# Retention and masked expert attention: the attention of each tile one step later, the projections spread over three steps, the output tiles moved

## The chip, the cores and the metric

The kernel runs on one core of one Trainium2 chip. The metric is the time of one execution on the device in microseconds (us), lower is better; the median of three runs before the change is 471.17 us (469.44 to 471.55). The engines have short names in the rows: PE is TensorE (matmuls; PEld its weight loads), DVE is VectorE, ACT is ScalarE, POOL is GpSimd, SP issues the DMAs.

## The reference

Two layers follow one another. The first is retention, causal attention without softmax, for 8 batches, 8 heads, 576 tokens and a head width of 64. The second takes its output (576 tokens, width 512) through four experts, each a causal softmax attention of width 64, and sums the two experts that a gate picks for each token.

```
scores = scale * (q @ k.T) * Dmat          # Dmat[i, j] = gamma_h ** (i - j) for j <= i, else 0
x = (scores @ v), heads side by side       # (8, 576, 512)

logits = x @ w_gate                        # 4 experts, best 2 kept, softmax over the 2
for e in range(4):
    q, k, v = x @ wq[e], x @ wk[e], x @ wv[e]
    a = softmax(causal(scale * q @ k.T))
    out += weight_of(e) * (a @ v @ wo[e])  # weight 0 where e is not picked
```

## The kernel before

The loop has 37 steps, n = 0 to 36. One step makes 128 rows of retention output for one pair of batches; nine steps (a period) make a pair, so there are four periods. Each engine runs its instructions strictly in the order in which the program emits them. There are 8 PSUM banks, handed out in turn: a new matmul result takes the bank that was handed out eight results earlier, and PE waits until that one was copied out.

A step emits, in this order. `factors` of the tiles scored one step earlier (DVE: softmax sum, reciprocal, times the gate's weight). `qk(n)` (two banks, copied out by ACT at L127, masked by POOL at L130). `result(n - 1)` and `state(n)`: PE makes `old` (two banks, copied out by ACT at L153), `own` (two banks, added by DVE at L171) and `st` (two banks, added by DVE at L113). What `own` gave goes through POOL (L176, L181) and ACT (L179), which split it into a high part `xh` and a low part `xl`, the input of the second layer. Then `scores` of this step's tiles: PE fills the banks `ss` (L352, L358), DVE takes the row maxima (L367, L371), ACT first scales the tiles of the step before (L393) and then does the exponentials (L375). Only after them does ACT come to `xh` (L179) of this step. Then `gates(0)` (first half of a gate, DVE and one ACT exponential), and at last the step's share of `work`, with the transposes (`turn`, DVE, L401 and L403) of the tiles scored one step earlier beside it.

A tile (b, t) is 128 rows of batch b in the second layer, t = 0 to 4. Tables say which step does what. `TILES` gives the tiles to score. `STEPS` gives the work, and its kinds are

- `kq` (R, p): the key and query projections of the block R of 384 rows for the expert pair p, 24 matmuls `pj` (L224). They read `xh` and `xl` of three steps; there are three blocks in a period
- `v` R: the value projection, three units of 12 matmuls `pv` (L249) that also give the gate's logits
- `back`: DMAs that bring values back in another layout
- `y` b: the attention times the values for a whole batch (`values`, `ys`, L415, four banks at a time, copied out by ACT L421 and DVE L422). In a step with a `y` the transposes are held until its end, because they write what `y` reads
- `o` c: one output tile (`outproj`, `po`, L437, one bank). ACT copies it out (L443), or DVE where c is in `FAST` (L441)

A gate has two halves: `gates(0)` after the scores of a step, `gates(1)` (L303 to L312, DVE) at the end of the step. The `factors` of the tiles need the gate's weights. After step 36 `tail` finishes the last pair by hand. I write steps by their residue: step 0 of a period is n = 9, 18, 27, 36.

Of the kernel before, what the change touches and what calls it, by code (L numbers as in the profile page):

```python
# [23 lines left out]
NP = B // 2  # L24
NC = 9 * NP
NB = 384

LAG = 6


def f(ap):
    return ap.bitcast(F32)
# [3 lines left out]
def kernel(ctx: ExitStack, tc: tile.TileContext, xf, vkf, wraw,  # L36
# [161 lines left out]
    def weights(n, parts="hl"):  # L198
        o, kc, w = WCUT[n]
        raw = RAW[n]  # L200
        wt = w if n != "v" else NWV
        if "h" in parts:
            W[n] = [const.tile([128, kc, wt], F32R, name="w" + y + n) for y in "hl"]
        hi, lo = W[n]
        for r, cs in [(raw, slice(0, w))] + ([(rg, slice(w, wt))] if n == "v" else []):
            if "h" in parts:
                act(hi[:, :, cs], r, AF.Copy)
            if "l" in parts:
                (gp if n == "q" else v).tensor_sub(lo[:, :, cs], r, f(hi[:, :, cs]))

# [235 lines left out]

    FAST = {9 * P_ + c for P_ in range(NP) for c in (1, 2, 3)}

# [3 lines left out]
    for P_ in range(NP):  # L452
        b, n = 2 * P_, 9 * P_
        for t in range(5):
            TILES.setdefault(n + 6 + t, []).append((b, t))
            TILES.setdefault(n + 10 + max(t, 1), []).append((b + 1, t))

        def add(m, *w):
            STEPS.setdefault(n + m, []).extend(w)
        R = 3 * P_  # L460
        add(4 - (P_ == 0), ("kq", R, 0))
        add(5 - (P_ == 0), ("kq", R, 1))
        add(5, ("v", R))
        add(7, ("kq", R + 1, 0))
        add(8, ("kq", R + 1, 1), ("v", R + 1))
        add(9, ("kq", R + 2, 0))
        add(10, ("kq", R + 2, 1), ("v", R + 2))
        add(8, ("back", R))
        add(10, ("back", R + 1))
        add(13, ("back", R + 2))  # L470
        add(12, ("y", b))
        add(13, ("o", n))
        add(15, *[("o", n + c) for c in (1, 2, 3)])
        add(16, ("y", b + 1))
        add(18, ("o", n + 4))
        add(20, ("o", n + 5), ("o", n + 6))
        add(21, ("o", n + 7), ("o", n + 8))
    for n in STEPS:
        first = "o" if n % 9 == 0 else "k"
        STEPS[n].sort(key=lambda x: (x[0][0] != first, "kvyob".index(x[0][0])))  # L480

    def work(n):
# [3 lines left out]
        i = 0  # L486
        for kind, *w in todo:
# [10 lines left out]
            elif kind == "v":  # L498
                for t in range(3):
                    yield from vproj(w[0], t)  # L500
            elif kind == "o":
                for y in vals:
                    next(y, None)
                yield from outproj(w[0])
# [6 lines left out]
    def run(g):  # L511
        for _ in g:
            pass
# [11 lines left out]
    def tail():  # L525
# [3 lines left out]
        def outs(*cs):  # L529
            for c in cs:  # L530
                yield from outproj(c)

        factors(b, 3)
        soft = scores((b, 4))
# [5 lines left out]
        beside(proj(R, "q", 1), turns)  # L540
        gates(0)
        gates(1)
        factors(b, 4)
        soft = scores((b + 1, 0), (b + 1, 1))
        next(soft)
        run(scale(b, 4))
        back(R - 1)
        beside(vproj(R, 0), soft)
        beside(vproj(R, 1), soft)
# [54 lines left out]
    for n in range(NC + 1):  # L604
        if n < LAG:
            load(n + 2)
        if n == 1:
            nc.sync.dma_start(rg, wraw[:, 4096:].rearrange("p (k w) -> p k w", k=4))
            nc.sync.dma_start(mask[:, 448:], con_d[:, 92:])
        if n in (1, 4):  # L610
            fetch("v" if n == 1 else "o")
        late = result(n - 1) if 1 <= n <= NC else iter(())
        now, old = TILES.get(n, []), TILES.get(n - 1, [])
        for x in old:
            factors(*x)
# [24 lines left out]
        run(late)  # L640
        for w in {2: "kq", 3: "v", 6: "o"}.get(n, ""):
            weights(w, "l" if w == "k" else "hl")
# [5 lines left out]
        run(turns)  # L648
        gates(1)
    tail()  # L650
# [52 lines left out]
```

## Time and profile before

| what | value |
|---|---|
| median of 3 runs | 471.17 us |
| profiled execution, whole | 474.0 us |
| its span, first to last instruction | 472.2 us |
| PE busy | 415.5 us, 88% |
| ACT, DVE, POOL busy | 279.8, 273.8, 170.4 us |
| granted TensorE clock, mean | 0.941 |

The profile is of one execution. "Busy" is the time in which an engine ran at least one instruction. The granted clock is the share of TensorE's full speed (2.4 GHz) that the chip gave; the two levels in the rows are 1.00 and 0.50 (1.2 GHz). In a row of the timeline the bracket behind an instruction tells how long its engine sat idle before it and what ended the idle time.

### The profile page before, as it was taken

To read this page: it belongs to the slowest core of one execution; us is meant where nothing else is said; L and a number is where in the kernel's file an instruction comes from. 1 tells how busy PE (TensorE), PEld (TensorE's weight loads), DVE (VectorE), ACT (ScalarE), POOL (GpSimd) and SP (SyncE) were. 2 spreads that over 40 slices of the span, in tenths; PEclk is the share of its full clock that TensorE was granted. 3 is DMA by queue.
4 is the path that set the end of the run, shared out by engine and by line. 5 is a ranking of instruction groups with operands and counts; after the bars stand their busy time and mean duration, and the time that the engine had idled before them with its cause. 6 is when DMAs were issued, how large, how long until landed. Compare 5 with 4: busy or idle time off the path is not lost.

```text
span 472.2 us, 20318 instructions
## 1 busy us (share of the span) xinstructions
PE 415.5 (88%) x8724; PEld 350.4 (74%) x8724; DVE 273.8 (58%) x1113; ACT 279.8 (59%) x798; POOL 170.4 (36%) x183
## 2 busy tenths in 40 slices
PE   6579796996899997997899998997999999899774
PEld 3469685995798786986698787895789678787563
DVE  2852765557775465657485564558385753673840
ACT  2545496566666366567495466568396456575651
POOL 1517673344354343344254433344264522100000
PEclk9669899898899999898999999899999999899988
DMA  8836654363444354454364444355264321313311
GB/s 285 325 92 226 214 144 138 111 148 117 121 151 147 136 144 140 136 153 150 111 207 121 162 143 134 107 145 196 91 177 134 117 64 35 89 58 110 118 68 47
DMA packets 33689, 65.10 MB, mean 138 GB/s; under 512 B 3392, under 2 KB 19264, under 8 KB 33600
## 3 DMA queue, kind: packets, MB, share of 16 engines
q1 hardware_dynamic: 33600, 63.80, 42.9%
q8 instruction: 69, 1.13, 1.0%
q14 instruction: 20, 0.16, 0.1%
HBM read 49.63 MB, written 14.16 MB: 135 GB/s over the span
## 4 chain that ended last, share of the span: by engine, by line
PE 67%; DVE 17%; ACT 9%; issue 4%; DMA 2%; POOL 0%; SPq 0%; DVEq 0%; ACTq 0%
PE pj L224 24%; PE ys L415 13%; PE pv L249 10%; PE po L437 6%; PE ss L352 4%; PE qk L124 3%; ACT p L375 3%; DVE p L367 2%; DVE x L171 2%; DVE s L113 2%; PE own L166 2%; PE st L106 2%; ACT x L153 2%; DVE ta L401 2%; DMA vk<-vkf 2%
## 5 line engine op out<-in xcount | busy, mean ns | idle before, releaser
L130 POOL TENSOR_SCALAR_AFFINE_SELECT p<-p 64x512 f32<-64x512 f32 x72 | 49.4, 687 | 120.0 <-ACT p L127 117.3
L375 ACT ACTIVATE p<-p,nm 128x64 f32<-128x64 f32 (+5 forms) x144 | 79.2, 552 | 15.6 <-DVE nm L367 9.8
L393 ACT ACTIVATE p<-p,sm 128x64 f32<-128x64 f32 (+5 forms) x144 | 69.4, 563 | 26.3 <-DVE sm L387 16.0
L171 DVE TENSOR_TENSOR x<-x,own 128x256 f32<-128x256 f32 (+1 forms) x72 | 25.5, 387 | 71.6 <-ACT x L153 70.9
L181 POOL TENSOR_TENSOR xl<-x,xh 128x512 fp32r<-128x512 f32 x33 | 42.3, 1283 | 61.0 <-ACT xh L179 61.0
L176 POOL TENSOR_TENSOR x<-x,gi 128x512 f32<-128x512 f32 x33 | 42.7, 1295 | 33.8 <-ACT p L393 18.1
L422 DVE TENSOR_TENSOR yl<-ys,yh 128x288 fp32r<-128x288 f32 (+2 forms) x36 | 12.8, 417 | 67.5 <-ACT yh L421 67.5
L367 DVE CUSTOM_DVE_ANT_0 p<-ss,mask 128x128 f32<-128x128 f32 (+7 forms) x128 | 50.6, 451 | 0.9 <-PE ss L352 0.8
L415 PE MATMUL ys<-ta,vq 32*64 32x192 f32 (+5 forms) x1152 | 43.0, 383 | 8.8 <-DVE x L171 6.3
L401 DVE STREAM_TRANSPOSE ta<-p 128x256 f32<-128x256 f32 (+2 forms) x144 | 49.0, 367 | 0.9 <-ACT p L393 0.9
L415 PEld LDWEIGHTS ys<-ta,vq 32*64 32x64 f32 x1152 | 31.8, 144 | 20.6 <-DVE x L171 8.8
L352 PE MATMUL ss<-k,q 64*64 64x512 f32 (+7 forms) x512 | 41.6, 423 | 3.4 <-ACT p L127 3.4
L224 PE MATMUL pj<-xh,whk 128*128 128x384 f32 x96 | 26.6, 405 | 14.4 <-ACT xh L179 14.4
L224 PEld LDWEIGHTS pj<-xh,whk 128*128 128x128 f32 x96 | 18.0, 214 | 27.0 <-ACT xh L179 16.8
L106 PE MATMUL st<-vk 64*64 64x64 f32 x1024 | 26.8, 228 | 7.2 <-DVE vk L95 2.7
L166 PE MATMUL own<-p,vk 64*64 64x64 f32 x1152 | 28.0, 228 | 5.6 <-issue 5.5
L253 ACT ACTIVATE vn<-pv 128x260 f32<-128x260 f32 x36 | 13.7, 386 | 30.9 <-PE pv L249 29.9
L127 ACT ACTIVATE p<-qk 128x256 f32<-128x256 f32 x72 | 23.8, 384 | 13.2 <-PE qk L124 12.5
L95 POOL TENSOR_TENSOR vk<-vk,con 128x512 f32<-128x512 f32 x30 | 31.5, 1050 | 0.0
L106 PEld LDWEIGHTS st<-vk 64*64 64x64 f32 x1024 | 22.5, 141 | 8.7 <-DVE ot L441 2.9
L166 PEld LDWEIGHTS own<-p,vk 64*64 64x64 f32 x1152 | 24.1, 140 | 6.4 <-issue 6.2
L124 PE MATMUL qk<-x 64*64 64x64 f32 x1152 | 26.3, 228 | 2.6 <-issue 2.6
(86 smaller groups left out, 906.9 us busy)
## 6 DMA issues: line engine op xcount, KB each, us to landing
x<-xf SPq DMA_DIRECT2D x36, 512.0 KB, 4.3
vk<-vkf SPq DMA_DIRECT2D x36, 512.0 KB, 5.8
vq<-hv SPq DMA_DIRECT2D x48, 192.0 KB, 6.7
out<-ot SPq DMA_DIRECT2D x36, 256.0 KB, 2.2
hv<-vn SPq DMA_DIRECT2D x24, 192.0 KB, 3.5
ta<-wraw SPq DMA_DIRECT2D x4, 512.0 KB, 8.0
gi<-gi SPq DMA_DIRECT2D x1, 256.0 KB, 7.9
con<-con SPq DMA_DIRECT2D x1, 46.0 KB, 3.0
```

Source lines behind the costliest of these rows:

```text
L106: mm(ps[r][HALF[g], s, u], vk[HALF[r], s, 1, h], vk[HALF[r], s, 0, h], start=True, stop=True)
L130: gp.affine_select(w, w, pattern=[[0, 8], [1, 64]], base=0, channel_multiplier=-1, compare_op=OP.is_ge, fill=0.0)
L166: mm(own[r][HALF[u], g, i], vk[HALF[r], s, 0, 2 * g + u], p[HALF[r], g, s, u], start=True, stop=True)
L176: e.tensor_mul(x32, x32, gi[:, :, t0:t0 + 128])
L224: mm(ps, ww[:, kc, p * 128:(p + 1) * 128], xx[:, kc], start=(i == 0), stop=(i == 11))
L249: mm(ps, xx[:, kc, l0:l0 + 128], ww[:, kc], start=(i == 0), stop=(i == 11))
L352: mm(ps[u][HALF[p]], q(p, z, i), k[p][HALF[z], :ws[u]], start=True, stop=True)
L367: v.tensor_tensor_reduce(x, ps[u], mask[:, 512 - ws[u]:], -1.0, BIG, OP.add, OP.min, nm[:, u:u + 1])
L375: act(x, x, AF.Exp, bias=bias, scale=-1.0, accum_out=sm[:, 0, u:u + 1])
L393: act(x, x, AF.Copy, scale=sm[:, 1, u:u + 1])
L401: v.transpose(TA[:, :min(nb, 8), z, k], x[:, :min(nb, 8)])
L415: mm(py[g][HALF[z], sj - s0:], vq[QUAD[g], jj, D * z:D * z + D], tt[QUAD[g]], start=(j == 0), stop=(j == 2 * s1 - 1))
```

## The change

Tiles are scored one step later (`LAG`). The three `v` units of a block, which stood behind the block's last `kq`, become single entries: block R in step 6, R+1 in step 0, R+2 in steps 1 and 2; the `kq` of R+2 move from steps 0 and 1 to steps 1 and 2. `y` moves from steps 3 and 7 to steps 4 and 8, each now beside a `kq`. Output tiles move to steps 0, 3 (four of them), 5, 6 and 7. The second half of a gate is emitted at the start of the following step ahead of its `factors`, instead of at the end of the step; nothing of DVE stands between these two places. At the start of the kernel the low part of one weight moves from POOL to DVE, and the `v` and `o` weights are loaded one step later. In the last pair ACT copies out three output tiles that DVE copied, and DVE one that ACT copied. The tail gains one step of scoring and one `kq`.

```
-LAG = 6
+LAG = 7
-                (gp if n == "q" else v).tensor_sub(lo[:, :, cs], r, f(hi[:, :, cs]))
+                v.tensor_sub(lo[:, :, cs], r, f(hi[:, :, cs]))
-    FAST = {9 * P_ + c for P_ in range(NP) for c in (1, 2, 3)}
+    FAST = {9 * P_ + c for P_ in range(NP - 1) for c in (1, 2, 3)} | {NC - 2}
-            TILES.setdefault(n + 6 + t, []).append((b, t))
-            TILES.setdefault(n + 10 + max(t, 1), []).append((b + 1, t))
+            TILES.setdefault(n + LAG + t, []).append((b, t))
+            TILES.setdefault(n + LAG + 4 + max(t, 1), []).append((b + 1, t))
-        add(5, ("v", R))
+        add(5 if P_ == 0 else 6, ("v", R, 0), ("v", R, 1))
+        add(6, ("v", R, 2))
         add(7, ("kq", R + 1, 0))
-        add(8, ("kq", R + 1, 1), ("v", R + 1))
-        add(9, ("kq", R + 2, 0))
-        add(10, ("kq", R + 2, 1), ("v", R + 2))
-        add(8, ("back", R))
-        add(10, ("back", R + 1))
-        add(13, ("back", R + 2))
-        add(12, ("y", b))
-        add(13, ("o", n))
-        add(15, *[("o", n + c) for c in (1, 2, 3)])
-        add(16, ("y", b + 1))
+        add(8, ("kq", R + 1, 1))
+        add(9, ("v", R + 1, 0), ("v", R + 1, 1), ("v", R + 1, 2), ("back", R))
+        add(10, ("kq", R + 2, 0), ("v", R + 2, 0))
+        add(11, ("kq", R + 2, 1), ("v", R + 2, 1), ("v", R + 2, 2), ("back", R + 1))
+        add(13, ("y", b))
+        add(14, ("o", n), ("back", R + 2))
+        add(15, ("o", n + 1))
+        add(16, ("o", n + 2), ("o", n + 3))
+        add(17, ("y", b + 1))
         add(18, ("o", n + 4))
-        add(20, ("o", n + 5), ("o", n + 6))
-        add(21, ("o", n + 7), ("o", n + 8))
+        add(21, *[("o", n + c) for c in (5, 6, 7, 8)])
-        first = "o" if n % 9 == 0 else "k"
-        STEPS[n].sort(key=lambda x: (x[0][0] != first, "kvyob".index(x[0][0])))
+        STEPS[n].sort(key=lambda x: "kvyob".index(x[0][0]))
...
-                for t in range(3):
-                    yield from vproj(w[0], t)
+                for _ in vproj(*w):
+                    i += 1
+                    if i == 3 and bring:
+                        back(bring.pop())
+                    yield
...
+        factors(b, 2)
+        soft = scores((b, 3))
+        next(soft)
+        run(scale(b, 2))
+        run(soft)
+        gates(0)
+        turns = turn(b, 2)
+        beside(proj(R, "k", 0), turns)
+        beside(proj(R, "q", 0), turns)
+        gates(1)
         factors(b, 3)
...
-        gates(0)
-        gates(1)
+        back(R - 1)
+        run(vproj(R, 0))
         factors(b, 4)
         soft = scores((b + 1, 0), (b + 1, 1))
         next(soft)
         run(scale(b, 4))
-        back(R - 1)
-        beside(vproj(R, 0), soft)
...
-        if n in (1, 4):
-            fetch("v" if n == 1 else "o")
+        if n in (2, 5):
+            fetch("v" if n == 2 else "o")
...
+        gates(1)
         for x in old:
             factors(*x)
...
-        for w in {2: "kq", 3: "v", 6: "o"}.get(n, ""):
+        for w in {2: "kq", 4: "v", 7: "o"}.get(n, ""):
...
-        gates(1)
```

What this does to PE in step 0 of the third period (n = 18), behind the step's `st`. Before, the output tile comes first and then the projection of block R+2:

```order
L352 MATMUL ss<-k_2242,q_2802 64x448 x2
L352 MATMUL ss<-k_2243,q_2803 64x448 x2
L352 MATMUL ss<-k_2242,q_2802 64x512 x2
L352 MATMUL ss<-k_2243,q_2803 64x512 x2
L437 MATMUL po<-who,yh 128x512 x2
L437 MATMUL po<-wlo,yh 128x512 x2
L437 MATMUL po<-who,yl 128x512 x2
L224 MATMUL pj<-xh,whk 128x384 x4
L224 MATMUL pj<-xh,wlk 128x384 x4
```

After:

```order
L352 MATMUL ss<-k_2046,q_2048 64x320 x2
L352 MATMUL ss<-k_2047,q_2049 64x320 x2
L352 MATMUL ss<-k_2046,q_2048 64x384 x2
L352 MATMUL ss<-k_2047,q_2049 64x384 x2
L249 MATMUL pv<-whv,xh 128x260 x4
L249 MATMUL pv<-wlv,xh 128x260 x4
L249 MATMUL pv<-whv,xl 128x260 x4
```

The values of block R+1, whose `xh` was made in earlier steps, stand where the projection stood that reads the `xh` of this very step; two more such units and the output tile follow.

In step 3 of the same period (n = 21) before, PE goes from the scores to `y`; one step earlier it had two output tiles:

```order
L106 MATMUL st<-vk 64x64 x16
L352 MATMUL ss<-k_2800,q_3342 64x320 x2
L352 MATMUL ss<-k_2801,q_3343 64x320 x2
L352 MATMUL ss<-k_2800,q_3342 64x384 x2
L352 MATMUL ss<-k_2801,q_3343 64x384 x2
L415 MATMUL ys<-ta,vq 64x288 x16
L415 MATMUL ys<-ta,vq 64x256 x16
```

After, the same scores stand in step 4 (n = 22), and a projection's first third stands ahead of `y`; one step earlier PE has four output tiles:

```order
L106 MATMUL st<-vk 64x64 x8
L352 MATMUL ss<-k_2739,q_3432 64x320 x2
L352 MATMUL ss<-k_2740,q_3433 64x320 x2
L352 MATMUL ss<-k_2739,q_3432 64x384 x2
L352 MATMUL ss<-k_2740,q_3433 64x384 x2
L224 MATMUL pj<-xh,whk 128x384 x4
L415 MATMUL ys<-ta,vq 64x288 x16
```

So two output tiles more and a third of a projection moved in between the scores of tiles 0 and 1 and the first matmul of `y`.

## Rows read from the trace of the kernel before

**Rows 1.** The page: the span, PE's busy time, and the granted clock in 40 slices of the span (in tenths).

```profile
span 472.2 us, 20318 instructions
PE 415.5 (88%) x8724; PEld 350.4 (74%) x8724; DVE 273.8 (58%) x1113; ACT 279.8 (59%) x798; POOL 170.4 (36%) x183
PEclk9669899898899999898999999899999999899988
```

**Rows 2.** The view of waits, PE alone: what waited for what, us in total, how often, the longest.

```profile
PE pj L224 <- ACT xh L179: 14.4, 5, 4.0
PE ys L415 <- DVE x L171: 6.3, 3, 2.7
PE own L166 <- issue: 5.5, 5, 2.5
PE ss L352 <- ACT p L127: 3.4, 2, 1.9
PE st L106 <- DVE ot L441: 2.5, 3, 0.8
```

**Rows 3.** Busy time by stretch: the steps 18, 20, 21 and 25. Columns: the stretch, its length, busy time of PE, PEld, DVE, ACT, POOL (with the count of instructions), granted clock, DMA share, GB/s.

```profile
180.78:194.34 13.56, 11.18 (x176) 9.17 (x175) 8.61 (x39) 8.01 (x21) 4.86 (x5) 0.87 0.39 129
205.85:211.99 6.14, 6.14 (x173) 4.96 (x172) 4.04 (x26) 5.31 (x20) 3.60 (x4) 1.00 0.62 178
211.99:230.12 18.13, 15.66 (x446) 12.37 (x445) 9.09 (x35) 10.32 (x32) 6.13 (x6) 0.91 0.35 125
259.31:275.53 16.22, 15.37 (x458) 12.34 (x457) 7.65 (x33) 6.30 (x23) 6.15 (x6) 1.00 0.34 122
```

**Rows 4.** The timeline at step 18, around PE's wait (start, length, engine, line, operation). The first row is the same wait in step 3, at the kernel's start.

```profile
28.26 1.65 PE L224 MATMUL pj<-xh,whk 128*128 128x384 f32 x4 [3.29 <-ACT xh L179]
...
183.73 1.28 POOL L176 TENSOR_TENSOR x<-x,gi 128x512 f32<-128x512 f32 x1
186.96 0.70 ACT L375 ACTIVATE p<-p,nm 128x512 f32<-128x512 f32 x1
187.85 0.61 ACT L179 ACTIVATE xh<-x 128x512 fp32r<-128x512 f32 x1
188.52 1.65 PE L224 MATMUL pj<-xh,whk 128*128 128x384 f32 x4 [2.38 <-ACT xh L179]
```

**Rows 5.** Busy time by stretch, columns as in rows 3: stretches right behind PE's waits in the steps 9, 18 and 21.

```profile
82.50:85.80 3.30, 3.30 (x11) 3.30 (x11) 2.80 (x15) 0.00 (x0) 1.11 (x1) 0.50 0.01 2
188.30:191.60 3.30, 3.08 (x10) 3.08 (x11) 3.05 (x16) 0.65 (x2) 1.27 (x1) 0.50 0.21 82
219.00:222.30 3.30, 3.30 (x52) 2.90 (x58) 2.44 (x12) 3.30 (x11) 2.27 (x2) 0.50 0.19 74
```

**Rows 6.** The timeline from step 20 into step 21: POOL, the gate's second half on DVE, then DVE's addition of `own`, and PE's first matmuls of `y`.

```profile
213.70 1.27 POOL L181 TENSOR_TENSOR xl<-x,xh 128x512 fp32r<-128x512 f32 x1 [2.60 <-ACT xh L179]
213.82 1.18 DVE L303 SCALAR_TENSOR_TENSOR ex<-rk,ex 128x12 f32<-128x12 f32 x1
218.12 0.75 DVE L171 TENSOR_TENSOR x<-x,own 128x256 f32<-128x256 f32 x2
218.60 5.26 PE L415 MATMUL ys<-ta,vq 32*64 32x288 f32 x96 [1.81 <-DVE x L171]
219.59 0.48 DVE L367 CUSTOM_DVE_ANT_0 p<-ss,mask 128x320 f32<-128x320 f32 x1
```

**Rows 7.** The same instruction of a gate on DVE at step 18, when POOL was idle, and the end of the factors behind it.

```profile
189.60 0.24 DVE L303 SCALAR_TENSOR_TENSOR ex<-rk,ex 128x12 f32<-128x12 f32 x1
191.61 0.16 DVE L387 TENSOR_TENSOR sm<-sm,wt 128x4 f32<-128x4 f32 x1
```

**Rows 8.** The timeline at step 16: DVE copies out an output tile, PE goes on with `st`.

```profile
153.34 0.65 DVE L441 COPY ot<-po 128x512 f32<-128x512 f32 x1
154.05 0.62 PE L106 MATMUL st<-vk 64*64 64x64 f32 x26 [0.83 <-DVE ot L441]
```

**Rows 9.** The timeline at step 7: ACT prepares a weight, then copies out `qk`, then PE gets on with the scores.

```profile
53.47 1.04 ACT L207 ACTIVATE who<-ta 128x1024 fp32r<-128x1024 f32 x1
54.83 2.04 PE L352 MATMUL ss<-k,q 64*64 64x192 f32 x16 [1.90 <-ACT p L127]
```

**Rows 10.** The chain that ended last, in order of time, around step 20: one whole `kq`, one whole `v` of three units, one output tile.

```profile
197.17 4.43 PE pj L224 x24
201.60 4.32 PE pv L249 x36
223.86 1.59 PE po L437 x6
```

**Rows 11.** Code loads: the DMA queue of instructions over the whole span (packets, MB, share of 16 engines), the same in the four us from 119, and PE's wait in that stretch.

```profile
q8 instruction: 69, 1.13, 1.0%
q8 instruction: 1, 0.02, 1.8%
122.82 0.62 PE L150 MATMUL old<-x,s 64*64 64x64 f32 x25 [1.58 <-issue]
```

**Rows 12.** The timeline at step 3: POOL makes a weight's low part, DVE beside it, and the same DVE instruction of the next step.

```profile
20.30 2.45 POOL L209 TENSOR_TENSOR wlq<-ta,whq 128x1024 fp32r<-128x1024 f32 x1 [0.29 <-POOL p L130]
20.47 2.83 DVE L95 TENSOR_TENSOR vk<-vk,con 128x512 f32<-128x512 f32 x1
...
26.27 0.67 DVE L95 TENSOR_TENSOR vk<-vk,con 128x512 f32<-128x512 f32 x1
```

## The prediction

> **What bounds the kernel now.** I read the page first. PE is busy for 415.5 of 472.2 us, the other engines for 280 us or less [rows 1]: PE is the bound, and a gain must come out of the 57 us in which it waits or out of the slices in which the clock row falls below 9. The work of PE is the same before and after; the change only puts it in another order. So the question is which waits go and which come.
>
> The view of waits says for what PE waits [rows 2]. Three kinds repeat with the period. Projections `pj` wait for `xh`, 14.4 us in five waits. `y` waits for DVE's addition L171, 6.3 us in three. `st` waits for an output tile's copy on DVE, 2.5 us in three. Beside them stands "issue", a wait for nothing that the profile shows.
>
> The stretches by step place them [rows 3]. Step 18 has 13.56 us and PE is busy for 11.18; step 21 has 18.13 and 15.66; step 20 is full, but only 6.14 us long. Step lengths are that uneven while each step brings ACT and DVE about the same scores.
>
> The timeline of step 18 shows the first kind [rows 4]. POOL has the row block ready at 185.01, but `xh` stands behind the exponentials on ACT, which run until 187.66, and PE starts its projection at 188.52 after 2.38 us of waiting. The projection reads the `xh` of this very step. In steps 9, 18, 27 and 36 it is the same; with step 3's 3.29 us taken off, the four waits are 14.4 - 3.3 = 11.1 us.
>
> Then the clock [rows 5]. Behind each of these waits, and behind the `y` waits, lies a stretch with the granted clock at 0.50, that is 1.2 GHz, with PE busy nearly throughout. 3.3 us at half speed do the work of 1.65 us, so such a wait costs 1.65 us more than its row says.
>
> **The change, part by part.**
>
> *The projection of R+2 leaves step 0.* In its place stand three `pv` units, whose input was finished two steps earlier, and they take 4.32 us [rows 10]; the projection stands one step later, when `xh` is long there. The four waits go: 11.1 us, and 4 x 1.65 = 6.6 us of half clock. Term: -17.7. If the projection found another late input there, nothing would be gained; I see none, since `xh`, `xl` and the weights are all older than a step.
>
> *`y` one step later, behind four output tiles.* What makes `y` wait is DVE: scores of two tiles, half a gate, transposes, the second half of the gate and two sets of factors stand ahead of the L171 that frees the banks. L171 starts at 218.12, 12.3 us after step 20 began at 205.85 [rows 3, 6]. Step 20 has 6.14 us, so PE gets there early. After, the step with these scores has two more output tiles, 2 x 1.5 us (1.59 for one alone in [rows 10]), and lasts 9.1 us. In step 21 PE asks for the first freed bank 4.8 us after the step's start (218.60 - 1.81 - 211.99), with about 0.5 us of an "issue" wait in it; after, a projection asks for it at 9.1 + 4.3 = 13.4 us, when DVE is 1 us ahead. The later banks, which `y` needs, are ready when DVE reaches L367, 1.5 us after L171 [rows 6], and the third of a projection ahead of `y` (4.43/6 = 0.7 us) covers more of that. So the two waits of 6.3 - 2.7 = 3.6 us in steps 21 and 30 go, with two half clocks, 3.3, and half of the 1 us over which the banks of `y` came free, twice. In the first period there are no output tiles yet to lengthen the step, so the 2.7 us of step 12 stay, in step 13. Term: -7.9; bounds -9 (step 12 helped too) and -3 (only half of it, and the clock still falls).
>
> *Output tiles.* Three copies on DVE stood at the end of step 6, and `st` of step 7 waits 0.83 us for the last [rows 8]. After, one stands in step 6 and two in step 7, behind a projection. Term: -2.5; bounds 0 and -4.
>
> *First period.* In step 7 PE waits 1.90 us because ACT makes the `o` weight (1.04 us) ahead of `qk`'s copy [rows 9], and a half clock follows. After, that weight stands in a step with a whole `kq` behind the scores, 4.43 us of cover [rows 10]. Term: -1.9 - 1.65 = -3.5; without the cover nothing.
>
> *The low part of wq on DVE.* It took POOL 2.45 us, and DVE's L95, which starts beside it, took 2.83 us [rows 12]; the same instruction alone took 0.67. The Trainium skill, page "SBUF — State Buffer", section "Who interferes with whom", says that a DVE instruction with two SBUF inputs and a GpSimd instruction that reads SBUF hold the shared port in turn and the second one blocks; the rows agree, both end within 0.6 us of each other. DVE gains 2 us and takes on a subtraction that I estimate at 1.7 us, two thirds of POOL's 2.45. Term: -0.5, between 0 and -1 in a stretch that waits for other things too.
>
> *Tail.* Three copies go from DVE to ACT; DVE's transposes come 0.7 us earlier and ACT's scales a little later. Term -0.5, between +1 and -1.5.
>
> *Costs.* The `v` weights one step later on ACT and DVE, at the edge of their use in step 5: +0.4. The gate's second half keeps its neighbours on DVE, since nothing stood between its two places; but in the shorter steps around it DVE has less room: +1, bounds 0 and the first rival. The wait on the single value buffer `vn` that v's first unit in step 1 could make is covered, because the DMAs that read it started a step earlier. "Issue" waits I leave at their size (second rival).
>
> Sum: -17.7 - 7.9 - 2.5 - 3.5 - 0.5 - 0.5 + 1.4 = -31.2 us. The profiled execution took 474.0 us, 1.8 more than its span and 2.8 more than the median of the runs. 474.0 - 31.2 = 442.8; against the median, 471.2 - 31.2 = **440 us**.
>
> **Rivals.**
>
> *DVE takes over* (chance 0.15). At step 20 the first instruction of a gate's second half took 1.18 us while POOL ran L181 beside it [rows 6]; at step 18 with POOL idle it took 0.24, and from there to the end of the factors it is 2.2 us [rows 7] against 4.3 us from 213.82 to L171 at 218.12. So 2.1 us can come on top wherever POOL runs beside it. After, that piece stands at the start of steps 2, 4 and 8, always near POOL's instructions. I gave step 4 its long form already. If steps 2 and 8 get it too, and 1 us of it is covered, PE waits 1.1 us and may lose 1.65 to the clock, six times: +16, 456 us. The page's rule, by which the blocked one waits for the whole instruction, is what makes this rival; by it this is the likely form wherever the two meet. For it speaks the row, against it that DVE is less busy in step 25 (7.65 of 16.22 us) than in step 21 [rows 3].
>
> *ACT takes over* (0.08). In step 3 ACT has eight exponentials and four copies, some 10 us in a step of 9.1. If it is late, PE waits for `qk`'s copy as in step 7 and step 12 (3.4 us in two waits [rows 2]): 1.5 + 1.65 in three periods, +9.5, 449 us.
>
> *Code loads set the end, slower than before* (0.04). PE's code comes in 69 packets [rows 11]. One falls into the stretch from 119 to 123, and there PE waits 1.58 us for nothing visible. If the denser order exposed every packet, each at 0.5 us more, that would be +34.5: 474.5 us, slower by 0.7%. It decides from 0.5 us a packet. For it speaks that "issue" makes PE's third longest group [rows 2]; against it that the steps with projections run full (step 20 too), and that `y` after the change alternates with long matmuls. The Trainium skill, page "Runtime: NRT & Kernel Launch", section "Instruction fetch mechanics", says that crossing a block of code is mostly hidden; by it this rival would be nothing, but this trace shows the 1.58.
>
> *More is gained* (0.05): the "issue" waits behind `y` shrink as well and step 12's wait goes: below 431.
>
> *Nothing changes* (0.02): the removed waits were only one of two late inputs, and PE meets the second at the same time.
>
> **How the numbers follow.** The forecast has 0.66, its own range 431 to 448. With both rivals of a slow engine the range reaches to 457 and leaves out 0.05 below and some 0.08 above. A measurement of this kernel can tell 0.5% (2.4 us) from no change. Faster: 0.66 + 0.15 + 0.08 + 0.05, less 0.01 for mixtures of the rivals, is 0.93; same 0.03; slower 0.04.
>
> **What would show it.** In the profile of the changed kernel, `pj` waiting for `xh` falls from 14.4 us to about 3.3, that of step 3. The clock row has some six slices fewer below 9 after the first quarter. Steps 18, 27 and 36 are full. `y` in steps 22 and 31 starts without a wait over 1 us, and step 13 still has one near 2.7 us. `st` behind DVE's output copies is gone from the waits. The prediction is wrong if PE's idle time in the span stays above 45 us, if new waits for L171 show in the steps 11, 17, 20 or 26, or if "issue" grows beyond 20 us.

## The result, and the profile after

The changed kernel takes 439.14 us (median of 4 runs, 436.44 to 441.74) beside 470.31 us for the kernel before: a ratio of 0.9345, 95% interval 0.9265 to 0.9424. A repeat gave 439.86 us and 0.9358 (0.9321 to 0.9395). That is 31 us less, and the forecast was 440 us. Ratios, here and below, leave out the executions that fell into a slower state of the chip, medians do not. The profiled execution took 436.4 us, so the two profiled executions lie 37.6 us apart: 474.0 is the longest execution of its kernel in this set and 436.4 the shortest of its own.

First the page of the changed kernel: span, busy time, and the granted clock in 40 slices (the counterpart of [rows 1]).

```profile
span 434.6 us, 20327 instructions
PE 399.9 (92%) x8724; PEld 334.0 (77%) x8724; DVE 272.2 (63%) x1112; ACT 277.8 (64%) x800; POOL 166.8 (38%) x182
PEclk9759999998999999999999999999999999999987
```

PE's idle time falls from 56.7 to 34.7 us (span less busy). Its busy time falls too, by 15.6 us with the same 8724 matmuls: time at half clock was busy time. From the fourth slice on, three slices stand below 9, where there were ten.

The waits of PE (the counterpart of [rows 2]); columns: what waited, for what, us in total, times, the longest.

```profile
PE own L166 <- issue: 5.0, 5, 2.2
PE pj L224 <- DVE x L171: 4.0, 4, 2.7
PE pj L224 <- ACT xh L179: 2.8, 1, 2.8
PE st L106 <- POOL vk L95: 1.3, 1, 1.3
PE ss L352 <- ACT p L127: 0.6, 1, 0.6
```

The projection waits for `xh` only in step 3. `st` behind DVE's output copies is gone. `y` no longer waits for L171; the projection that now stands ahead of it does, 2.7 us of the 4.0 in step 13. The repeat has 4.6 us in all, 0.66 of them in step 22.

Busy time by stretch of the steps 18, 20, 21 and 22, columns as in rows 3.

```profile
162.79:172.94 10.15, 9.42 (x187) 8.09 (x186) 7.66 (x32) 7.42 (x23) 4.88 (x5) 1.00 0.71 182
182.21:192.53 10.32, 10.32 (x193) 9.65 (x192) 7.75 (x33) 7.44 (x17) 4.89 (x5) 1.00 0.63 179
192.53:201.80 9.27, 9.21 (x186) 7.13 (x185) 7.10 (x34) 8.39 (x28) 4.89 (x5) 1.00 0.55 164
201.80:216.16 14.36, 14.22 (x441) 11.44 (x441) 5.78 (x27) 8.62 (x26) 4.88 (x5) 1.00 0.42 147
```

Where steps lay between 6.14 and 18.13 us, these lie between 9 and 15, at full clock and with 0.93 us of PE's idle time in all four.

The timeline of step 18 after (the counterpart of [rows 4]): PE's value units, then ACT's `xh`; and the projection in the next step, which has no bracket.

```profile
167.05 0.74 PE L249 MATMUL pv<-whv,xh 128*128 128x260 f32 x4
169.88 0.62 ACT L179 ACTIVATE xh<-x 128x512 fp32r<-128x512 f32 x1
...
176.37 0.97 PE L224 MATMUL pj<-xh,whk 128*128 128x384 f32 x4
```

`xh` of this step still comes some 3 us after PE is through with the scores, but nothing reads it before 176.37.

The timeline from step 21 into step 22 (the counterpart of [rows 6]): POOL and the gate's second half on DVE, L171, and PE's first matmuls of the projection and of `y`.

```profile
200.39 1.29 POOL L181 TENSOR_TENSOR xl<-x,xh 128x512 fp32r<-128x512 f32 x1 [2.62 <-ACT xh L179]
200.49 1.22 DVE L303 SCALAR_TENSOR_TENSOR ex<-rk,ex 128x12 f32<-128x12 f32 x1
204.56 0.74 DVE L171 TENSOR_TENSOR x<-x,own 128x256 f32<-128x256 f32 x2
205.03 0.97 PE L224 MATMUL pj<-xh,whk 128*128 128x384 f32 x4
205.92 1.45 PE L415 MATMUL ys<-ta,vq 32*64 32x288 f32 x35
```

### The profile page after: what moved, and what is told of

It reads as the page before. It is cut to its first block, busy times and chain, and to the rows that moved or that the text cites. A ratio compares the mean times of both kernels' runs of the same rounds, so it can differ in the third digit from the quotient of the medians.

```text
span 434.6 us, 20327 instructions
## 1 busy us (share of the span) xinstructions
PE 399.9 (92%) x8724; PEld 334.0 (77%) x8724; DVE 272.2 (63%) x1112; ACT 277.8 (64%) x800; POOL 166.8 (38%) x182
## 5 line engine op out<-in xcount | busy, mean ns | idle before, releaser
L393 ACT ACTIVATE p<-p,sm 128x64 f32<-128x64 f32 (+5 forms) x144 | 69.5, 561 | 22.7 <-DVE sm L387 18.6
L130 POOL TENSOR_SCALAR_AFFINE_SELECT p<-p 64x512 f32<-64x512 f32 x72 | 48.2, 670 | 88.2 <-ACT p L127 85.8
L181 POOL TENSOR_TENSOR xl<-x,xh 128x512 fp32r<-128x512 f32 x33 | 42.5, 1287 | 60.1 <-ACT xh L179 60.1
L171 DVE TENSOR_TENSOR x<-x,own 128x256 f32<-128x256 f32 (+1 forms) x72 | 25.5, 386 | 35.4 <-ACT x L153 34.5
L352 PE MATMUL ss<-k,q 64*64 64x512 f32 (+7 forms) x512 | 38.2, 406 | 0.6 <-ACT p L127 0.6
L415 PE MATMUL ys<-ta,vq 32*64 32x288 f32 (+5 forms) x1152 | 36.0, 355 | 1.3 <-DVE ta L401 1.3
L415 PEld LDWEIGHTS ys<-ta,vq 32*64 32x64 f32 x1152 | 24.7, 134 | 11.9 <-issue 3.8
L421 ACT ACTIVATE yh<-ys 128x288 fp32r<-128x288 f32 (+2 forms) x36 | 10.9, 388 | 32.7 <-PE ys L415 32.7
L95 POOL TENSOR_TENSOR vk<-vk,con 128x512 f32<-128x512 f32 x30 | 31.5, 1049 | 0.0
L224 PEld LDWEIGHTS pj<-xh,whk 128*128 128x128 f32 x96 | 16.4, 197 | 18.9 <-PE ss L352 5.5
L224 PE MATMUL pj<-xh,whk 128*128 128x384 f32 x96 | 24.4, 378 | 6.9 <-DVE x L171 4.0
L179 ACT ACTIVATE xh<-x 128x512 fp32r<-128x512 f32 x36 | 22.3, 618 | 11.2 <-POOL x L176 7.1
L106 PE MATMUL st<-vk 64*64 64x64 f32 x1024 | 25.1, 225 | 4.5 <-issue 1.7
L124 PEld LDWEIGHTS qk<-x 64*64 64x64 f32 x1152 | 21.2, 138 | 9.1 <-issue 7.6
```

What stands on the lines that cost most here:

```text
L95: (gp if n > 5 else v).tensor_mul(vv, vv, gam[:, k:k + 2].unsqueeze(3).to_broadcast([128, 2, 4, D]))
L124: mm(ps[g][HALF[r], s, u], x[HALF[g], 1, h, i], x[HALF[g], 0, h, i], start=True, stop=True)
L130: gp.affine_select(w, w, pattern=[[0, 8], [1, 64]], base=0, channel_multiplier=-1, compare_op=OP.is_ge, fill=0.0)
L181: e.tensor_sub(xl[:, :, l0:l0 + 128], x32, f(xh[:, :, l0:l0 + 128]))
L224: mm(ps, ww[:, kc, p * 128:(p + 1) * 128], xx[:, kc], start=(i == 0), stop=(i == 11))
L352: mm(ps[u][HALF[p]], q(p, z, i), k[p][HALF[z], :ws[u]], start=True, stop=True)
```

## The experiments

Each time is a median of an experiment's executions, and each ratio is against executions of the kernel before on the same chip. "Changed" stands for the changed kernel, 439.1 and 439.9 us in two sets of runs.

### What the late projection cost

The first three move `kq` of block R+2.

`e1_xh_first`, from the changed kernel:

```
-        add(9, ("v", R + 1, 0), ("v", R + 1, 1), ("v", R + 1, 2), ("back", R))
-        add(10, ("kq", R + 2, 0), ("v", R + 2, 0))
+        add(9, ("kq", R + 2, 0), ("v", R + 1, 0), ("v", R + 1, 1), ("v", R + 1, 2), ("back", R))
+        add(10, ("v", R + 2, 0))
```

(the tail then makes one `kq` less).

> The changed kernel with one thing put back: the key and query projection kq(R+2, 0) stands in step 0 of a period again, ahead of the v units; in step 1 only v stays. All work is the same. Theory of the late input: the projection reads the xh of this very step, so PE waits for ACT's xh four times again (steps 9, 18, 27, 36), 2.4 to 4 us each as in the kernel before, with a half clock behind each: pj behind xh rises from 2.8 to about 13 us, and the time by 14 to 18 us, to about 454. Rival, that only the even lengths of the steps matter: step 0 now has more work than before the change, so the wait is short or none, and the time rises by 0 to 4 us.

`e2_xh_last` is the same with the projection behind `v` and `o` in step 0:

```
-        STEPS[n].sort(key=lambda x: "kvyob".index(x[0][0]))
+        STEPS[n].sort(key=lambda x: ("vyobk" if n % 9 == 0 else "kvyob").index(x[0][0]))
```

> The same projection kq(R+2, 0) in step 0 as in the experiment before, but behind the three v units and the output tile of the step. Theory of the late input: 4.3 us of v and 1.5 us of an output tile cover the lateness of xh (2.4 to 4 us), so pj waits for xh stay near 2.8 us (step 3 alone) and the time stays within 4 us of the changed kernel. Rival, that it is the step that is wrong and not what stands ahead: plus 14 to 18 us as in the experiment before.

`e5_before_kq_later`, from the kernel before:

```
-        add(9, ("kq", R + 2, 0))
-        add(10, ("kq", R + 2, 1), ("v", R + 2))
+        add(10, ("kq", R + 2, 0), ("kq", R + 2, 1), ("v", R + 2))
```

> The kernel before with one part of the change alone: kq(R+2, 0) goes from step 0 to step 1, where kq(R+2, 1) and v stand already; in the tail both kq of the last block stand together. Theory (the prediction's first term): the four waits for xh and their half clocks go, 17.7 us less than the kernel before. Rival, that a step 0 with little work only moves the wait: step 0 has no long matmuls left, PE gets through it early and waits in step 1 for DVE's L171 or for ACT's copy of qk, and 8 us or less are gained.

Measured: e1 479.97 us (ratio 1.0237, 1.0188 to 1.0287), slower than the kernel before; e2 455.84 (0.9727, 0.9671 to 0.9784); e5 470.38 (1.0022, 0.9988 to 1.0055), no change. The theory of the late input alone fails in all three: e2 and e5 come out at the rival's numbers, e1 beyond both. The steps 18, 19 and 20 show why; first e1, then e2, columns as in rows 3 (changed: 10.15, 9.27 and 10.32 us, 29.7 together).

```profile
172.88:192.09 19.21, 15.08 (x211) 13.68 (x210) 7.63 (x32) 8.63 (x25) 4.86 (x5) 0.91 0.42 98
192.09:197.12 5.03, 5.03 (x142) 3.63 (x141) 3.53 (x15) 4.70 (x12) 3.42 (x4) 1.00 0.93 295
197.12:212.51 15.39, 12.36 (x193) 11.44 (x193) 12.22 (x52) 9.67 (x25) 6.30 (x7) 0.89 0.47 136
```

```profile
164.66:179.15 14.49, 13.65 (x211) 12.34 (x211) 7.73 (x32) 8.52 (x25) 4.88 (x5) 1.00 0.68 175
179.15:184.18 5.03, 5.03 (x141) 3.64 (x140) 3.53 (x15) 4.61 (x12) 3.42 (x4) 1.00 0.59 193
184.18:199.54 15.36, 12.36 (x193) 11.44 (x192) 12.21 (x52) 9.68 (x25) 6.30 (x7) 0.89 0.44 127
```

Two things are put back at once. One is the late `xh`: step 18 has 19.21 us in e1, and 14.49 in e2, where `v` and `o` stand ahead and the step is about as long as its work (10.15 us and a `kq` of 4.43 [rows 10]). The waits of PE for `xh` in the whole kernel say the same, e1 first:

```profile
PE pj L224 <- ACT xh L179: 21.2, 5, 5.3
PE pj L224 <- ACT xh L179: 3.2, 1, 3.2
```

The 3.2 us of e2 are those of step 3, which has 5.3 in e1. The other thing is the short step: step 19, without its projection, has only 5.03 us, so that PE is early in step 20, which takes 15.4 us in both. The timelines: e1 in step 18 and in step 20, then e2 in step 20.

```profile
180.61 1.65 PE L224 MATMUL pj<-xh,whk 128*128 128x384 f32 x4 [3.56 <-ACT xh L179]
203.68 0.68 PE L224 MATMUL pj<-xh,whk 128*128 128x384 f32 x2 [2.09 <-DVE x L171]
```

```profile
186.84 0.62 PE L106 MATMUL st<-vk 64*64 64x64 f32 x26 [0.92 <-ACT vn L253]
```

PE waits 3.56 us for `xh` in step 18 of e1, and in step 20 2.09 us for L171; in both kernels `st` also waits 0.9 us for ACT's copy of a value unit. So against the changed kernel e2 costs 16 us by the medians. Its profile lies 19.6 us above the changed kernel's: 3.5 to 5.3 us come from the steps 0 to 2 of each of three periods, which is the price of the short step, and 6.4 from the end, where the edit changes step 36 and the tail too. The late input costs another 24 us (e1 less e2): 15.7 us more idle time (60.5 against 44.8) and 7.6 us more busy time at half clock.

In e5 the late input is gone, but for 1.20 us in step 36, and nothing is won, because step 18, left with one output tile, has 5.28 us. Step 18 and 19 (before: 13.56 and 11.51), then PE's waits in step 19.

```profile
180.79:186.07 5.28, 5.28 (x152) 3.56 (x151) 3.25 (x13) 4.62 (x12) 3.59 (x4) 1.00 0.63 164
186.07:207.31 21.24, 18.15 (x213) 16.91 (x213) 12.39 (x54) 11.12 (x28) 6.11 (x6) 0.92 0.42 128
```

```profile
189.02 0.62 PE L106 MATMUL st<-vk 64*64 64x64 f32 x26 [1.45 <-ACT ot L443]
192.84 0.94 PE L224 MATMUL pj<-xh,whk 128*128 128x384 f32 x4 [1.63 <-DVE x L171]
```

The waits for ACT's output copy (1.45 us) and for L171 (1.63) take the place of the wait for `xh` (2.38). The changed kernel does both: it takes the projection away and gives step 0 three value units and step 1 a projection and a unit. The first half alone is worth nothing (e5). The second half alone was not run; e1 and e2 keep the units in step 0, but they leave step 1 short.

### What `y` waited for

`e6_before_outs_4`, from the kernel before:

```
-        add(20, ("o", n + 5), ("o", n + 6))
-        add(21, ("o", n + 7), ("o", n + 8))
+        add(20, *[("o", n + c) for c in (5, 6, 7, 8)])
```

> The kernel before with another part alone: four output tiles in step 2 of the periods 2 to 4 (steps 20, 29) instead of two in step 2 and two in step 3, ahead of the y that stands in step 3. Theory (the prediction's second term): with 3.1 us more in the short step, DVE is ahead when y asks for its banks; the y waits of steps 21 and 30 (3.6 us of 6.3) and their half clocks (3.3 us) go, 6 to 8 us less than the kernel before. Rival, that y has to stand beside a projection as well: no change, 0 to 2 us less.

`e3_outs_2_2`, from the changed kernel:

```
-        add(21, *[("o", n + c) for c in (5, 6, 7, 8)])
+        add(20, ("o", n + 5), ("o", n + 6))
+        add(21, ("o", n + 7), ("o", n + 8))
```

> The changed kernel with two of the four output tiles of step 3 put back into step 2 (steps 20 and 29), as the kernel before had them; y stays in step 4 behind a third of a projection. Theory of the short step: step 3 shrinks from 9.3 to about 6.2 us, PE gets to step 4 early and waits there for DVE's L171 in steps 22 and 31, 1 to 2 us each with a half clock behind it: 5 to 8 us more. Rival, that y only had to stand a step later and behind the piece of a projection: no change, within 2 us.

Measured: e6 465.1 us (0.9891, 0.9824 to 0.9959), 5.1 us less by the ratio; e3 442.42 (0.9375, 0.9319 to 0.9431), by the ratio 1.4 us over the changed kernel, with intervals that overlap. The profile of e3 is of its longest execution, so only waits are read from it. The timeline at `y`: L171 and PE, first e6 (step 21), then e3 (step 22), and the stretch behind e3's wait, columns as in rows 3.

```profile
215.15 0.75 DVE L171 TENSOR_TENSOR x<-x,own 128x256 f32<-128x256 f32 x2
215.62 4.33 PE L415 MATMUL ys<-ta,vq 32*64 32x288 f32 x117 [0.43 <-DVE x L171]
```

```profile
215.27 0.75 DVE L171 TENSOR_TENSOR x<-x,own 128x256 f32<-128x256 f32 x2
215.74 0.96 PE L224 MATMUL pj<-xh,whk 128*128 128x384 f32 x4 [1.90 <-DVE x L171]
```

```profile
215.70:219.00 3.30, 3.26 (x87) 2.63 (x94) 2.49 (x11) 3.30 (x11) 2.28 (x2) 1.00 0.31 124
```

Counted from the start of the step in which DVE has the scores of two tiles, the numbers fall into one table:

| kernel, steps | PE asks for the bank | PE gets it | wait |
|---|---|---|---|
| before, 20 to 21 [rows 6] | 10.9 | 12.75 | 1.81 |
| e6, 20 to 21 | 12.3 | 12.70 | 0.43 |
| changed, 21 to 22 | 12.5 | 12.50 | 0 |
| repeat of changed, 21 to 22 | 12.1 | 12.73 | 0.66 |
| e3, 21 to 22 | 10.9 | 12.79 | 1.90 |
| changed, 12 to 13 | 9.8 | 12.47 | 2.71 |
| f2 (below), 12 to 13 | 10.3 | 12.49 | 2.17 |

DVE gives the bank 12.5 to 12.8 us after the step began, wherever `y` stands (all fourteen profiles have 12.3 to 12.8 at these places, but for 13.1 in `e8` below, where PE itself stood still for 3.4 us in step 13). Only work of PE in these 12.5 us decides. So the four output tiles, not the later step, take the wait away. In e3 the waits are back, as the theory says, but not their price: 1.4 us instead of 5 to 8 is the rival's number. The half clocks did not come: the clock behind its wait is 1.00, and in step 31, with 2.02 us, too.

### Output tiles, weights, and the length of step 6

`e4_outs_3_0`, from the changed kernel:

```
-        add(15, ("o", n + 1))
-        add(16, ("o", n + 2), ("o", n + 3))
+        add(15, *[("o", n + c) for c in (1, 2, 3)])
```

> The changed kernel with the three output tiles that DVE copies out all in step 6 again, none in step 7. Theory: st of step 7 waits again for the last of DVE's copies, 0.6 to 0.8 us in three periods, 2 to 4 us more in all. Rival: the waits come back but step 7, now shorter by two output tiles, leads into y in step 8 with DVE behind: waits for L171 there too, 5 us or more. Nothing at all if the copies were never what st waited for.

`f4_weights_early`, from the changed kernel:

```
-        if n in (2, 5):
-            fetch("v" if n == 2 else "o")
+        if n in (1, 4):
+            fetch("v" if n == 1 else "o")
-        for w in {2: "kq", 4: "v", 7: "o"}.get(n, ""):
+        for w in {2: "kq", 3: "v", 6: "o"}.get(n, ""):
```

> The changed kernel with the v and o weights fetched and prepared one step earlier again, as the kernel before had them. Theory (the prediction's term for the first period): the o weight's 1.04 us on ACT stand ahead of qk's copy again, PE waits about 1.9 us for it in step 7 with a half clock behind: 2 to 4 us more. Rival, that the shorter waits came from the other order of the work in steps 5 to 9: no change beyond 1 us.

`g1_v_step5` is e4 with all three value units of block R in step 5:

```
-        add(5 if P_ == 0 else 6, ("v", R, 0), ("v", R, 1))
-        add(6, ("v", R, 2))
+        add(5, ("v", R, 0), ("v", R, 1), ("v", R, 2))
```

> The changed kernel with the value units of block R all in step 5 again (also in the first period, where the change had put the last of them into step 6) and the three output tiles that DVE copies all in step 6, as in the kernel before; the weights stay one step later. Theory that a short step makes the waits, whatever stands at its end: step 6 has 2.2 us in the first period and about 7 us in the others, so ss waits about 1.9 us for ACT's copy of qk in step 7 with a half clock behind, though the weights are out of the way, and st waits 0.6 to 0.8 us for DVE's output copy in steps 16, 25 and 34: 4 to 7 us more than the changed kernel, 443 to 447. Rival, the prediction's own reasons (the o weight on ACT in step 6 made the first wait): step 7 stays without the wait for qk's copy, only the three waits of st return, 2 to 3 us more.

Measured: e4 438.38 us (0.9324, 0.9268 to 0.9379) and f4 439.40 (0.9347, 0.9312 to 0.9382), neither to be told from the changed kernel; g1 443.09 (0.9456, 0.941 to 0.9501), 3 to 4 us more by the medians and 5 by the ratio. The end of step 15 (residue 6): DVE's last output copy and the next `st`, first e4, then g1.

```profile
145.85 0.69 DVE L441 COPY ot<-po 128x512 f32<-128x512 f32 x1 [0.70 <-PE po L437]
147.27 0.62 PE L106 MATMUL st<-vk 64*64 64x64 f32 x28
```

```profile
148.26 0.65 DVE L441 COPY ot<-po 128x512 f32<-128x512 f32 x1
148.97 0.62 PE L106 MATMUL st<-vk 64*64 64x64 f32 x26 [0.60 <-DVE ot L441]
```

With three copies at the end of step 6 e4 has no wait, because the value units ahead of them make that step 11.78 us long and DVE has time left. Without the units (7.42 us) `st` waits 0.60 us, and again in steps 25 and 34. The wait for `qk`'s copy in step 7 is less clear. In f4 ACT makes the `o` weight at the end of step 6's work again, and PE does not wait for the copy. But it waits 1.91 us ahead of `st` before that, as the repeat of the changed kernel does (1.86), and the copy, which starts at 52.72, is made while PE waits until 53.33. So f4 does not show what the weight would cost without that wait. The view puts the wait down to POOL's L181 or L95; the rows of the changed kernel speak against it:

```profile
50.15 1.04 POOL L95 TENSOR_TENSOR vk<-vk,con 128x512 f32<-128x512 f32 x1
52.01 0.64 PE L106 MATMUL st<-vk 64*64 64x64 f32 x29 [1.31 <-POOL vk L95]
```

L95 had ended 0.8 us before PE went on (0.3 to 2.1 us before in the nine profiles with this order), and `st` does not read what L181 makes. A packet of PE's code fits all nine (see `f0` below). In g1, with the weight out of the way and step 6 1.92 us long, PE waits for `qk`'s copy after all (step 6 by stretch, then the timeline of step 7):

```profile
46.74:48.66 1.92, 1.92 (x129) 1.92 (x132) 0.00 (x0) 1.92 (x8) 1.55 (x2) 1.00 0.21 83
```

```profile
53.99 0.83 PE L352 MATMUL ss<-k,q 64*64 64x64 f32 x16 [0.70 <-ACT p L127]
```

but 0.70 us and at full clock, with a wait of 1.38 us ahead of it. In the kernel before the weight can have added no more than its 1.04 us [rows 9] to the wait of 1.90. So both theories had a part, and f4 and g1 do not divide it further.

`e7_wlq_pool`, from the changed kernel:

```
-                v.tensor_sub(lo[:, :, cs], r, f(hi[:, :, cs]))
+                (gp if n == "q" else v).tensor_sub(lo[:, :, cs], r, f(hi[:, :, cs]))
```

> The changed kernel with the low part of the query weight back on POOL. Theory (the prediction's term): 0 to 1 us more. What the profile of the changed kernel suggests instead: its half clock stretch at the start is 13.7 us long where the kernel before has 17.1; if the subtraction's place made that, the stretch is 17 us again and the time rises by 1.5 to 2.5 us, and the start of step 7 goes from 49.0 to about 51 us.

Measured 440.32 us (0.9338, 0.9285 to 0.9391): no difference. The half clock at the start is no sign of it either: it lasts 13.7 us in the first profile of the changed kernel and 17.1 in its repeat, as in e7, and step 4 begins between 33.3 and 35.6 us in nine profiles of the changed kernel and its variants, the changed kernel's own at 33.4 and 33.3, e7's at 34.4.

### The executions of one kernel, and two better versions

`f0_after_again` is the changed kernel unaltered.

> The changed kernel itself once more, beside the two runs that follow. Its executions so far lie between 436.4 and 441.7 us. Expectation: a median of 437 to 441 us. If the difference between its executions comes from PE's waits for nothing that the profile shows (in other versions with the same order a wait of 2.1 to 2.8 us of this kind stood ahead of st in step 10, which the first profile does not have) and from the start-up, a second profile differs there and nowhere in the later periods by more than 1 us.

Its runs lie between 434.37 and 440.95 us (median 439.86). Against the expectation the second profile (434.37) has no wait in step 10 either; step 15's wait for nothing visible is 0.30 us where it was 1.40. But five variants with the same instructions of PE there (f4 and g1 with small changes before it) have one. The timeline of e7 in step 10, and the DMA queue of PE's code (packets, MB, share of 16 engines) from 75.5 to 76.2 in e7 and from 71.5 to 72.2 in the changed kernel:

```profile
78.57 0.39 PE L106 MATMUL st<-vk 64*64 64x64 f32 x10 [2.21 <-issue]
```

```profile
q8 instruction: 1, 0.02, 11.9%
```

```profile
q8 instruction: 1, 0.02, 9.6%
```

Step 10 begins at 74.63 in e7 and at 73.68 in the changed kernel: the same code packet starts 1.3 us after the step began, or 1.5 us ahead of it. Over the nine profiles:

| start of the packet against that of step 10 | wait of `st` |
|---|---|
| changed, f0, e8: 2.0 to 1.0 us ahead | none |
| f2: 0.5 to 0 ahead | 0.57 |
| e4, e7, f4, g1: 1.0 to 1.5 behind | 2.0 to 2.3 |
| e3: 1.5 to 2.0 behind | 2.83 |

PE goes on 2.5 to 2.7 us after the start of the packet in all six that wait, and in step 7 it goes on 2.3 to 2.5 us after the start of another in all nine. The same holds for most waits for nothing visible: of the eleven in the changed kernel that are longer than 0.25 us, ten (13 us together) end 2.4 to 2.8 us after a code packet started, and the eleventh is the wait for `yh` below. That the packet is the cause is read from these times and was not tried by itself. The Trainium skill, page "Runtime: NRT & Kernel Launch", section "Instruction fetch mechanics", calls the crossing of a block mostly hidden; the rows agree for a packet that is early, and for a late one they show 2 to 2.8 us in the open. What makes it late in some executions was not tried either.

`e8_tail_y_first`, from the changed kernel, in the tail:

```
-        run(scale(b + 1, 3))
         run(values(b + 1, 0, 6))
+        run(scale(b + 1, 3))
```

> The changed kernel with one place of the tail in another order: the last but one group of attention times values is emitted ahead of the scales of tile 3 on ACT and not behind them. Theory: PE's wait of 3.0 us near 410 us, which stands for the yh that ACT makes only after the scales, goes and with it a half clock, while the transposes of tile 3 come some 2 us later behind other work: 1 to 3 us less. Rival: the transposes then end the tail later by as much as the wait was long: no change.

Measured 434.41 us (0.9235, 0.9193 to 0.9277), 5 us less than the changed kernel and more than the 1 to 3 expected. The timeline at that place, changed and then e8: the scales L393, `yh`, and PE's output tile.

```profile
410.39 2.43 ACT L393 ACTIVATE p<-p,sm 128x448 f32<-128x448 f32 x4
412.73 0.95 ACT L421 ACTIVATE yh<-ys 128x192 fp32r<-128x192 f32 x4
413.35 1.19 PE L437 MATMUL po<-who,yh 128*128 128x512 f32 x2 [3.04 <-issue]
```

```profile
411.06 0.97 ACT L421 ACTIVATE yh<-ys 128x192 fp32r<-128x192 f32 x4
411.68 0.89 PE L437 MATMUL po<-who,yh 128*128 128x512 f32 x2 [0.71 <-issue]
```

The wait that the profile puts down to nothing visible (3.0 us) was one for `yh` behind the scales; it falls to 0.7, and no half clock follows, where one stood from 413.1 on. Wait (2.3 us) and half clock (1.7) are 4 of the 5 us; the rest lies within the intervals.

`f2_v_step12`, from e8, takes two value units of the second period into step 12:

```
-        add(5 if P_ == 0 else 6, ("v", R, 0), ("v", R, 1))
+        add((5, 3, 6, 6)[P_], ("v", R, 0), ("v", R, 1))
```

> The changed kernel with the tail of the experiment before (one group of attention times values ahead of the scales of tile 3), and in the first period two value units of the next block (2.9 us of PE's work, input one and two steps old) in the short step 12 instead of step 15. Theory of the short step: step 12 has 3.0 us and DVE is behind in step 13, where PE waits 2.7 us for L171 and 0.6 us for ACT's copy of qk with a half clock behind; 2.9 us of work ahead cover these, so step 13 shrinks from 22 us to 17 to 19 and the time falls by 3 to 5 us against the version with the tail alone (434.4), to about 430. Rival: step 15 becomes the short one and the wait moves to step 16, or the one value buffer vn makes ACT wait in step 12: no gain.

Measured 432.99 us (0.9215, 0.9183 to 0.9248), the fastest, but not to be told from e8: 1.4 us less, where 3 to 5 were expected. The profile shows the gain: steps 12 to 15 take 40.9 us where e8 has 44.6 and f0 44.3, and step 16 gives 0.4 back. The wait for L171 is still 2.17 us in step 13, since PE asks after 10.3 us (table above); the units filled what had been a code wait and the wait for `qk`'s copy.

## Why the prediction was right, step by step

**What bounds.** PE did, and the gain came out of its idle time (22.0 us) and its half clock (15.6 us). Idle time is 34.7 us where 45 was the limit, and no new wait for L171 shows in the steps 11, 17, 20 or 26. "Issue" makes 16.5 us beside 17.3 before; 3.0 of these are the `yh` wait, of which e8 took 2.3 away.

**The projection (-17.7).** The size was right in the profile: 14.4 to 2.8 us of waits, and the four half clocks behind them. The reason was half of it. The text says that nothing would be gained if the projection found another late input, and sees none; e5 shows that the projection need not find one: with the late input removed alone, `st` and the projection of step 1 wait for ACT's copy and for L171 instead, and the gain is 0. What I put in one clause, that three value units stand in its place, was needed too: with a step left short, the gain is gone (e5) or 16 us of it are (e2).

**`y` (-7.9).** Mis-sized. The waits of DVE's L171 fell from 6.3 to 4.0 us, not to 2.7, and e6 measured 5.1 for this part alone on the kernel before, inside the bounds of 3 and 9. I had PE asking 13.4 us after the step's start, 1 us behind DVE. It was 12.5, level with it or up to 0.7 us ahead, and steps 13 and 31 kept 2.71 and 0.66. Of the sum 9.1 + 4.3 the first part held (9.27). The second was read in step 21, where `st` has 32 matmuls; in step 22 `st` has 16, and PE asks 3.2 us after that step's start. The 1 us was also counted from the start of L171, 12.3; the bank comes at 12.75 [rows 3, 6]. The mechanism, 12.3 us of DVE against PE's work, is the part that held best. Step 13's wait came as said.

**Output tiles (-2.5), first period (-3.5).** The waits went: `st` behind L441 from 2.5 us to 0, as summed; step 7's idle time from 3.00 to 1.31 us (1.86 in the repeat), with its half clock. But the steps of the sum that name the cause failed: splitting the output tiles (e4) and moving the `o` weight (f4) change nothing when undone. Beside e4, g1 only takes the value units out of step 6 again, and the waits return: these units did it for the output tiles. For the weight the cause stays open in part, since in f4 another wait covers its time. That other wait, 1.31 us of `st` in step 7, I had not seen; by its time it belongs to a code packet and not to POOL's L95.

**wlq, tail, costs.** wlq is 0 (e7), inside its bounds, though its parts came: the subtraction took DVE 1.21 us (1.67 in the repeat) where I estimated 1.7, and L95 took 0.68 where it had 2.83 beside POOL. The tail and the cost of +1.4 can't be told apart in these profiles.

**Half clock.** 1.65 us for each of seven stretches made 11.55; PE's busy time fell by 15.6. Gone beyond the seven are the stretch behind step 13's "issue" wait [rows 11] and 3.4 us of the stretch at the start (17.1 to 13.7), which the repeat has at full length; the tail keeps its three. These 4 us of lost clock and 2.3 us more of idle time than the sum has make the profiled executions lie 37.6 us apart and not 31.2. That the medians lie 31 us apart, as summed, is in part luck: terms that were too high and too low met, and a term like that of the projection is not what its move alone is worth.

**The rivals.** DVE did not take over: L303 takes 1.18 to 1.22 us beside POOL's L181 for the steps 13, 22 and 31, as it did before in three places, and 0.27 us or less elsewhere. I had read the 0.24 us of [rows 7] as the time with POOL idle. It was not idle:

```profile
188.54 1.27 POOL L181 TENSOR_TENSOR xl<-x,xh 128x512 fp32r<-128x512 f32 x1 [2.53 <-ACT xh L179]
```

L303 started at 189.60, when little was left of L181, and ended 0.02 us behind it. It ends 0.02 to 0.03 us behind L181 in all 13 places of the two profiles where the two meet; where no POOL instruction runs beside it, L303 takes 0.13 to 0.17 us. The Trainium skill, page "SBUF — State Buffer", section "Who interferes with whom", has the second of such a pair blocked; the rows agree (1.22 beside 1.29). The rival did not come because in step 2 L303 starts 0.25 us before the end of L181, and in step 8 after it. ACT did not: it is busy for 8.39 of the 9.27 us of step 21, and `ss` waits 0.6 us once (1.44 in the repeat). Code loads stayed at their size, by the "issue" waits of the profiles; what they make of the difference between executions is not shown. That nothing changes, because a second late input waits, is not what this change did, but it is what e5 did.

## What to carry to other kernels

A wait has two sides: what comes late, and that the waiting engine comes early. Before a wait is priced at its full length, add up for each step the work of the fast engine against the fixed chain of the slow one (here 12.5 us on DVE from a step's start to the freed bank), and move work until PE no longer gets there first. Undoing the parts one by one then shows prices that do not add up (here 40, 16, 4, 1, 0, 0 and 0 us against 31 for the whole). Here that was a sign that one cause, the uneven steps, stood behind several of them.

## What the runs showed of the hardware

A wait near 2 us may or may not bring PE to half clock, in one program at waits of one length. In e2 the same idle time, 3.0 us in two waits, stands in steps 11 and 20; the clock is the column ahead of the last two.

```profile
83.06:96.92 13.86, 10.83 (x194) 9.91 (x193) 12.23 (x52) 9.56 (x25) 6.36 (x7) 1.00 0.49 142
```

Step 11 runs at 1.00 and step 20 at 0.89 (row above), and takes 1.5 us more. Behind the single wait of 1.58 us in the kernel before [rows 11] a half clock came; behind one of 2.4 us (e6, step 18) none. What decides between them these runs do not show; as a price, 1.65 us behind each wait of 1.6 to 2.4 us was right for some and too much for others.
